# Talking-heads attention and a Fourier-mixing feed-forward: who issues the first loads, and the order of the first and last feed-forward units

## The chip, the cores and the metric

The kernel runs on one core of a Trainium2 chip. The metric is the device time of one execution in microseconds; the time of a kernel is the median of its runs.

## The reference

```python
# attention: 8 batches, 12 heads, 448 rows, 64 columns each
scores = scale * np.matmul(q, k.transpose(0, 1, 3, 2))
scores = np.einsum('bhij,hg->bgij', scores, w_pre)       # heads are mixed
attn = np.exp(scores - scores.max(-1, keepdims=True))
attn = attn / (attn.sum(-1, keepdims=True) + 1e-09)
attn = np.einsum('bhij,hg->bgij', attn, w_post)          # and mixed again
x = np.matmul(attn, v)                                   # to (8, 448, 768)
# Fourier mix and feed-forward
u = x + np.real(np.fft.fft(np.fft.fft(x, axis=1), axis=2))
un = (u - u.mean(-1)) / np.sqrt(u.var(-1) + 1e-06)
out = u + np.maximum(un @ w_ch1, 0.0) @ w_ch2            # 768 -> 3072 -> 768
```

All is float32; the two feed-forward weights come as 64-bit floats and are converted on the chip.

## The kernel before

**First phase (`mix_phase`).** Each batch is done in 23 steps, 184 in all; a step handles a few query rows of all 12 heads. Block by block (two or three steps a block), TensorE forms scores (`emit_qk`, "QK") out of transposed q and k (`emit_xpose`), one pair of head columns (`xx`) at a time, and ScalarE copies them to a tile `Sb` of which there are two. For each step, four DMAs gather rows of `Sb` into `Kr` (`emit_gather`, line 641), so that heads lie on partitions. TensorE mixes the heads (`emit_premix`), VectorE takes the maximum (`emit_max`), ScalarE the exponential (`emit_exp`), VectorE the reciprocal sum and GpSimd the scaling of `PP` (`emit_scale`, line 676); TensorE mixes again (`emit_postmix`), VectorE transposes to `Pv` (`emit_turn`), and TensorE multiplies by v (`emit_av`). Gathers run five steps ahead of the post-mix, premix to scaling two.

A list `fill` holds everything that is due at a step: `due(kind, at, fn)`. Steps below 0 are the prologue. The order of TensorE, VectorE, ScalarE and GpSimd in this phase is the order in which the program emits; SyncE mostly issues DMAs. Loads of the first batch (`b == 0`) are all due at step -40: for each of three pairs k, then q, each in four DMAs of 112 KB (line 570), two by SyncE and two by ScalarE, then v (line 579) by SyncE. Loads of later batches are GpSimd's, due at the steps of `AT_L` and `AT_V`. `emit_load_mix` loads the head-mixing weights `wrp` and a mask `mk`; `emit_mix` makes `kw1` and `kw2` of them.

The Fourier mix of a batch folds its rows on GpSimd (`fold`; tiles `xs`, `xq`, `xf`; lines 781 to 802) and finishes with small matmuls. Results are stored by closures that wait in a list `later`: some stores are indirect (line 864), and one of a single row follows (line 870). Converting the weights (`_Weights`; raw loads at line 232) is dealt out in small pieces (`wts.deal`) over all steps.

**Second phase (`ffn_phase`).** The 3584 rows are cut into 7 units of 512 rows, the hidden width into 6 parts, and each product is done in a seven-product scheme. For the first part, `first` computes the hidden values of a unit (line 1207, seven groups of 12 matmuls in the order of `ORDER`) and `second` multiplies by the second weights (line 1284) and adds to u. In between, the next unit is prepared: row statistics on VectorE (`stats`), their scales on GpSimd (`power`, four small operations on `mv`, lines 411 to 414), the normalization on ScalarE (`norm`, `un`, line 1136), transposes on TensorE (`turn`, line 1145). The unit n = 0 begins while the last pieces of the first phase are still done beside it (`next_part`, `fold_rest`). While unit 0 is emitted, GpSimd's order is the program's; from unit 1 on a scheduler places GpSimd's instructions.

For the other five parts, `second2` does each product once more in seven (line 1325) and adds quarters (128x192) of seven accumulators `D[j]` on ScalarE (copies, line 1353) and VectorE (adds, line 1347); whole accumulators are added to each other on 128x768 (`both`, line 1356) and go to `out` in DRAM by accumulating DMAs that GpSimd issues (`out_`, line 1359). In the very last unit (`end`) two quadrants of `out` are loaded into spare accumulators, completed there, and written by SyncE and ScalarE (`store`, line 1363). `on(s, fn)` places `fn` behind the s-th matmul pair of that list.

Of the kernel before, what the change touches and what calls it, by code (L numbers as in the profile page):

```python
# [16 lines left out]
P = 128  # L17
# [13 lines left out]
KR = R * NH  # L31
# [29 lines left out]
TOT = B * GS  # L61
# [27 lines left out]
AT_T = ((5, 9), (15, 16), (13, 15))  # L89
AT_L = ((-4, -3), (-2, -1), (0, 1), (2, 7), (10, 11), (12, 13))  # L90
AT_V = ((2, 3), (4, 5), (6, 7))
AT_QK = ((0, 2, 1), (0, 1, 2), (0, 1, 2), (1, 2, 2),
         (0, 1, 2), (0, 1, 2), (0, 1, 2), (0, 1, 2))
AT_AV = ((1, 2, 4), (0, 1, 3), (1, 3, 5), (1, 3, 4))
# [354 lines left out]
def mix_phase(ctx, tc, rest, ident, q, k, v, w_pre, w_post, u_scr, u_rev, wts, lead):  # L449
# [60 lines left out]
    def emit_load_mix():  # L510
        for t in dens:
            nc.gpsimd.memset(t[:, :, :], 1e-9)
        nc.gpsimd.memset(wrp[:, :, :], 0.0)
        nc.sync.dma_start(out=mk, in_=cn["mk"].ap())
        for x in range(2):
            for y in range(2):
                nc.sync.dma_start(
                    out=wrp[64 * x + 30 * y:64 * x + 30 * y + 30, 0, :],
                    in_=_ap(w_pre, 6 * y * NH, [[0, R], [NH, 6], [1, NH]]))
            nc.sync.dma_start(out=wrp[64 * x:64 * x + KR, 1, :],  # L520
                              in_=_ap(w_post, 0, [[0, R], [NH, NH], [1, NH]]))

    def emit_mix():
# [31 lines left out]
    def emit_load_qk(b, xx, nm, y):  # L555

        src = q if nm == "q" else k
        if y == 0 and b == 0 and xx == START[-1]:

            if "raw" not in first:  # L560
                first["raw"] = ppv.tile([P, GT, 2 * S], F32, name="Pv", tag="Pv")
            batches[b]["raw" + nm, xx] = first["raw"][:, nm == "q"].rearrange(
                "p (c x d) -> p c x d", c=C7, x=2)
        elif y == 0:
            batches[b]["raw" + nm, xx] = praw.tile([P, C7, 2, D], F32, name="raw" + nm,
                                                   tag="raw")
        t = batches[b]["raw" + nm, xx]
        for x in range(2):
            eng = nc.gpsimd if b else (nc.sync, nc.scalar)[x]
            eng.dma_start(  # L570
                out=t[64 * y:64 * y + 64, :, x, :],
                in_=src[b, 6 * y + 2 * xx + x].rearrange("(p c) d -> p c d", c=C7))
        return True

    def emit_load_v(b, pr, y):
        if y == 0:
            batches[b]["v", pr] = pvv.tile([P, 2, C7 * D], F32, name="vv", tag=f"vv{pr}")
        h = 6 * y + 2 * pr
        (nc.gpsimd if b else nc.sync).dma_start(
            out=batches[b]["v", pr][64 * y:64 * y + 64, :, :],  # L580
            in_=v[b, h:h + 2].rearrange("h (p c) d -> p h (c d)", c=C7))

# [49 lines left out]
    def emit_gather(T):  # L632

        Kr = pkr.tile([P, 2, S], F32, name="Kr", tag="Kr")
        n, j = at_step[T]
        Sb, rs = blocks[n]["Sb"], blocks[n]["rs"]
        row = _row(Sb)
        for z in range(2):
            for x in range(2):
                p0 = 64 - R * rs + 4 * j + 2 * z + x  # L640
                nc.sync.dma_start(
                    out=Kr[64 * x:64 * x + KR, z, :],
                    in_=_ap(Sb, p0 * row, [[rs * row, 2 * R], [S, 6], [1, S]]))
        steps[T]["Kr"] = Kr
# [242 lines left out]
    for b in range(B):  # L887
        f = b * GS
        at_t = [(a, nm, xx) for xx, at in enumerate(AT_T) for nm, a in zip("qk", at)]
        if b == 0:  # L890

            for i, xx in enumerate(START):
                for j, nm in enumerate("kq"):
                    for y in range(2):
                        due("none", -40, lambda xx=xx, nm=nm, y=y: emit_load_qk(0, xx, nm, y))
                    due("full", 2 * i + j - 20, lambda xx=xx, nm=nm: emit_xpose(0, xx, nm))
                for n in range(2):
                    due("QK", 2 * i + 2 + n - 20, lambda n=n, xx=xx: (emit_qk(n, xx), n))
            for pr in range(3):
                for y in range(2):  # L900
                    due("none", -40, lambda pr=pr, y=y: emit_load_v(0, pr, y))
        else:
            for at, (a, nm, xx) in zip(AT_L, sorted(at_t, key=lambda e: e[0])):
                for y in range(2):
                    due("none", f + at[y] - GS,
                        lambda b=b, xx=xx, nm=nm, y=y: emit_load_qk(b, xx, nm, y))
            for xx, at in enumerate(AT_T):
                for nm, a in zip("qk", at):
                    due("full", f + a - GS,
                        lambda b=b, xx=xx, nm=nm: emit_xpose(b, xx, nm))  # L910
        for pr in range(3 if b else 0):
            for y in range(2):
                due("none", f + AT_V[pr][y], lambda b=b, pr=pr, y=y: emit_load_v(b, pr, y))
        for n in range(0 if b else 2, NBL):
            for xx in range(3):
                due("QK", f + BLOCK_AT[n] - 8 + AT_QK[n][xx],
                    lambda n=NBL * b + n, xx=xx: (emit_qk(n, xx), n))
        for n in range(NG):
            for pr in range(3):
                due("AV", f + GROUP_AT[n + 1] + AT_AV[n][pr],  # L920
                    lambda a=b * NG + n, pr=pr: (emit_av(a, pr), None))
            at, gi = AT_X[n]
            if b == B - 1 and n > 1:
                at += 2
            due("full", f + at, lambda g=groups[b * NG + gi]: emit_x(g))
        for n, at in enumerate(AT_Z):
            due("full", f + at, lambda b=b, n=n: emit_z(b, n // 2, n % 2))
        for pair in range(2):
            for par in range(2):
                due("full", f + AT_S[pair][par],  # L930
                    lambda b=b, pair=pair, par=par: emit_s2(b, pair, par))
# [8 lines left out]
    due("none", f + 15, lambda: lead.power(lead.mv))  # L940
    due("none", f + 26, lambda: lead.total(0))
    due("none", 0, lambda: wts.deal(0))
    due("none", -39, emit_load_mix)
    due("none", -3, emit_mix)
    for at, t in ((9, (rows, "at", 0, PN)), (16, (ts, "ts", 0, PN)),
                  (17, (tcs, "tc", 0, CW // 2)), (19, (tcs, "tc", CW // 2, CW))):
# [21 lines left out]
    with tc.manual_schedule(engines={ET.PE, ET.DVE, ET.Activation, ET.Pool}):  # L968
        while s <= TOT - GS + AT_X[-1][0]:
# [3 lines left out]
            for op in ORDERS[s % 2]:  # L973
# [12 lines left out]
                elif op == "scale":  # L986
                    if ahead:
                        emit_scale(s + LM)
                    for _ in range(old):
                        later.pop(0)()  # L990

                    if s < TOT - 3:
# [43 lines left out]
TOTALS = ((4, 6, 0), (5, 2, 4), (6, 2, 6), (3, 1, 5))  # L1036
DEEP = 1
HALVES = {0: ((0, 0),), 1: ((1, 1), (2, 0)), 2: ((3, 1),), 3: ((4, 0),), 4: ((5, 1), (6, 0))}
DEALS = ((2, 2, 2, 2, 2, 0, 0), (3, 4, 4, 4, 3, 0, 0))
DEST = {0: (0, 0), 1: (0, 0), 4: (1, 1), 5: (0, 1), 2: (0, 1), 6: (1, 1), 3: (1, 0)}  # L1040
ACC = {0: "P", 5: "P", 6: "P", 3: "P", 1: "Q", 4: "R", 2: "R"}
# [3 lines left out]
def ffn_phase(ctx, tc, rest, ident, u_scr, u_rev, wts, ub_scr, out, fold_rest,  # L1045
# [135 lines left out]
    def first(n, st, beside):  # L1181
# [12 lines left out]
        for k, i in enumerate(ORDER):  # L1194
# [39 lines left out]
                nc.scalar.activation(h21, h21, ACTF.Relu)  # L1234
            else:
                nc.scalar.activation(h12, p, ACTF.Relu)
            x = k - 2 * (n == 0)
            if norms and 0 <= x < NT2:
                stats(t + 1, x)
                if x == NT2 - 1:  # L1240
                    power(t + 1)
            if (n == 0 and k < 2) or (n == 1 and k not in (1, 2)):
                next_part()
                if n == 0 and k == 1:
                    fold_rest(8)
            if n == 0 and k == 5:
                fold_rest()
            if deep:
# [22 lines left out]
    def second(t, st):  # L1271
# [6 lines left out]
        for k, i in enumerate(ORDER):  # L1278
# [18 lines left out]
                total(t + 1, k - NT2 + 1)  # L1297
            if t == 0 and k > 2:
                next_part()
            wts.deal(2 if norms and k >= NT2 else 4)  # L1300
            if t == NTB - 1:
                load_w2(1, i)

    def second2(n, st):
# [61 lines left out]
        for j, i in enumerate(ORDER2):  # L1366
# [7 lines left out]
                if key:  # L1374
                    on(b + s, take, j, q, key)
            on(b + 6, take, j, 0, "Q")
            on(b + 11, more, j, 3, "P")
            on(b + 16, more, j, 1, "R")
            if t == NTB - 1 and c + 1 < NC:
                on(b + 17, load_w2, c + 1, i)  # L1380
        j0, j3, j5, j6, j4, j1, j2 = range(7)
        v11, v12 = 7, 8
        pl = nc.gpsimd
        on(12, lambda: quarters(vec, st["hq"], st["h"], H21, H21 + 1))
        on(19, lambda: quarters(vec, st["hq"], st["h"], HS1, HS1 + 1))
# [1 line left out]
                                         st["h"][:, HS2], op=ALU.subtract))  # L1387
        on(20, lambda: quarters(pl, st["hq"], st["h"], H12S, H12S + 1))
        if end:
            for v, r, d in ((v11, 0, 0), (v12, 0, 1)):  # L1390
                on(0, load, v, r, d)
            on(27, out_, j3, 1, 0)
            for s, *o in ((24, vec, v11, j0), (33, vec, j5, j0), (34, pl, v12, j5),
                          (40, vec, j6, j5), (45, vec, v12, j4), (46, vec, j4, j6),
                          (52, vec, v11, j1)):
                on(s, both, *o)
            on(41, out_, j6, 1, 0)
            on(47, out_, j4, 1, 1)
            on(53, store, v11, 0, 0)
            on(61, store, v12, 0, 1)  # L1400
        else:
            for s, *o in ((33, j5, j0), (40, j6, j5), (47, j5, j4), (54, j0, j1),
                          (61, j5, j2), (62, j4, j6)):
                on(s, both, vec, *o)
            on(27, out_, j3, 1, 0)
            on(44, out_, j6, 1, 0)
            on(55, out_, j0, 0, 0)
            on(62, out_, j5, 0, 1)
            on(63, out_, j4, 1, 1)
# [14 lines left out]
    fold_rest()  # L1424
    parts_ = [(c, k) for c in range(1, NC) for k in range(NK + FM)]
    for n in range(NTB):
        if n:
            wts.add(*parts_.pop(0))
        wts.deal(0)
        if n + 2 < NTB:  # L1430
# [4 lines left out]
            for i in ORDER:  # L1435
                nc.sync.dma_start(out=ub_scr[0][i], in_=lead.ub[i])
        second(n, st)
        wts.deal(1000)
        if n == 0:
            order.close()  # L1440
            order.enter_context(tc.manual_schedule(engines={ET.PE, ET.DVE}))
# [100 lines left out]
```

## Time and profile before

| | us |
|---|---|
| median of 3 runs | 2321.06 |
| lowest, highest | 2319.83, 2324.16 |
| the profiled execution's own time | 2313.94 |
| span of its records | 2312.0 |

The profiled execution is 7.1 us below the median. The table of engines, in us of the span:

| engine | busy |
|---|---|
| TensorE (PE) | 2251.5 (97%) |
| VectorE (DVE) | 1719.8 (74%) |
| GpSimd (POOL) | 1277.2 (55%) |
| ScalarE (ACT) | 1170.2 (51%) |

A row of the timeline reads: start in us, length in us, engine, line, operation, what is written and read, how many, and in brackets how long the engine had been idle and what ended it. Rows with SPq or ACTq are DMA issues, whose length is that of the issuing. The attention steps and the Fourier mix run to some 808 us, the feed-forward from there to the end.

### The profile page before, as it was taken

The numbers are of one execution on the slowest core, as the hardware profiler recorded it, in microseconds if no ns is written. First come the engines' busy times: TensorE is split into PE (matmuls) and PEld (weight loads), VectorE is DVE, ScalarE is ACT, GpSimd is POOL, SyncE is SP. The second block draws the span as 40 slices with busy tenths as digits, with TensorE's granted clock in tenths as the row PEclk, the third lists the DMA queues.
The fourth block names the chain that finished last, engine by engine and source line by source line (L and its number), as shares of the span: only waits on it lengthen the run. The fifth ranks groups of instructions, "written<-read, shape, count | busy, mean of one in ns | idle before, by whom it ended". The sixth has DMA issues, their size and how long they took to land.

```text
span 2312.0 us, 60775 instructions
## 1 busy us (share of the span) xinstructions
PE 2251.5 (97%) x22894; PEld 1738.0 (75%) x22894; DVE 1719.8 (74%) x3628; ACT 1170.2 (51%) x3336; POOL 1277.2 (55%) x1784
## 2 busy tenths in 40 slices
PE   6999999999999999999999999999999999999998
PEld 2455555555555677676899999999999899999997
DVE  3878878888877857777777787878778877765545
ACT  4776767666676622221345445444444445434433
POOL 3587868878787632221555454556555645453333
PEclk9999999999999999999999999999999999999999
DMA  7575655657656375667777887878777977795664
GB/s 162 163 187 163 187 176 164 195 159 192 186 172 197 134 249 196 205 205 285 219 172 194 226 229 187 222 180 248 209 185 188 281 182 176 190 259 120 141 144 69
DMA packets 231904, 439.04 MB, mean 190 GB/s; under 512 B 39608, under 2 KB 154064, under 8 KB 231614
## 3 DMA queue, kind: packets, MB, share of 16 engines
q1 hardware_dynamic: 157902, 302.97, 38.1%
q0 software_dynamic: 67856, 130.43, 29.9%
q8 instruction: 183, 3.00, 0.6%
q10 hardware_dynamic: 5856, 1.77, 0.5%
q14 instruction: 107, 0.88, 0.1%
HBM read 212.76 MB, written 143.16 MB: 154 GB/s over the span
## 4 chain that ended last, share of the span: by engine, by line
PE 83%; POOL 4%; DVE 4%; DMA 3%; ACT 2%; issue 1%; SPq 1%; ACTq 0%; DVEq 0%; POOLq 0%
PE psP L1207 17%; PE psP L1325 13%; PE psR L1207 9%; PE psR L1325 7%; PE mx L652 6%; PE ms L716 5%; PE ms L624 5%; PE po L686 4%; PE psQ L1207 4%; PE psQ L1325 3%; PE psP L1284 3%; PE ms L841 2%; PE psR L1284 1%; DMA Kr<-Sb 1%; PE ms L598 1%
## 5 line engine op out<-in xcount | busy, mean ns | idle before, releaser
L1359 POOL DMA_DIRECT2D out_dram<-od x173 | 210.1, 1273 | 262.8 <-DVE od L1347 187.2
L676 POOL TENSOR_SCALAR PP<-PP,rcp 128x448 f32<-128x448 f32 x368 | 235.2, 649 | 194.5 <-DVE rcp L674 164.9
L666 ACT ACTIVATE PP<-mx,nmx 128x448 f32<-128x448 f32 x368 | 230.5, 632 | 169.4 <-DVE nmx L659 156.7
L659 DVE TENSOR_REDUCE nmx<-mx 128x1 f32<-128x448 f32 x368 | 212.5, 618 | 92.8 <-PE mx L652 89.3
L1170 POOL TENSOR_TENSOR hq<-h 128x128 f32<-128x128 f32 (+1 forms) x210 | 129.7, 618 | 256.9 <-ACT h L1229 124.2
L1353 ACT COPY od<-psP 128x192 f32<-128x192 f32 x488 | 156.4, 320 | 171.9 <-PE psP L1325 170.7
L1356 DVE TENSOR_TENSOR od<-od 128x768 f32<-128x768 f32 x210 | 201.3, 972 | 52.1 <-ACT od L1353 51.8
L624 PE MATMUL ms<-kT,qT 64*32 64x448 f32 (+1 forms) x3072 | 199.3, 548 | 13.7 <-ACT qT L487 6.1
L487 ACT COPY Sb<-ms 124x448 f32<-124x448 f32 (+1 forms) x384 | 184.7, 541 | 54.3 <-PE ms L624 26.6
L699 DVE STREAM_TRANSPOSE Pv<-po 128x896 f32<-128x896 f32 x184 | 203.7, 1107 | 5.8 <-PE po L686 5.2
L652 PE MATMUL mx<-Kr,kw 60*32 60x448 f32 x2944 | 195.0, 550 | 8.8 <-ACT PP L666 5.0
L686 PE MATMUL po<-PP,kw 60*32 60x448 f32 x2944 | 187.8, 539 | 2.8 <-issue 1.4
L716 PEld LDWEIGHTS ms<-Pv,vv 64*64 64x64 f32 x5376 | 137.6, 132 | 69.8 <-issue 45.7
L1207 PE MATMUL psP<-qs,w1t 128*128 128x256 f32 x744 | 179.1, 379 | 0.8 <-DVE h L1228 0.8
L1207 PE MATMUL psP<-ks,w1t 128*128 128x256 f32 x744 | 179.1, 379 | 0.1
L716 PE MATMUL ms<-Pv,vv 64*64 64x120 f32 (+1 forms) x5376 | 159.7, 263 | 0.6 <-DVE XT L749 0.4
L252 POOL TENSOR_SCALAR wst<-wst 128x256 f32<-128x256 f32 (+1 forms) x76 | 118.2, 1564 | 67.9 <-ACT wst L263 66.6
L1207 PEld LDWEIGHTS psP<-qs,w1t 128*128 128x128 f32 x744 | 139.4, 190 | 17.6 <-DVE h L1228 1.2
L1207 PEld LDWEIGHTS psP<-ks,w1t 128*128 128x128 f32 x744 | 139.4, 190 | 16.7 <-DVE u L1289 0.7
L1207 PE MATMUL psP<-ub,w1t 128*128 128x256 f32 x528 | 127.1, 379 | 1.1 <-DVE h L1228 1.1
L1228 DVE TENSOR_TENSOR h<-h,psP 128x512 f32<-128x512 f32 x42 | 28.8, 686 | 127.6 <-PE psP L1207 104.9
L1325 PE MATMUL psP<-w2t,hq 128*128 128x192 f32 x490 | 122.4, 332 | 1.2 <-DVE od L1347 1.2
(190 smaller groups left out, 5289.2 us busy)
## 6 DMA issues: line engine op xcount, KB each, us to landing
Kr<-Sb SPq DMA_DIRECT2D x736, 105.0 KB
out_dram<-od POOLq DMA_DIRECT2D x173, 384.0 KB, 6.3
qs<-ub SPq DMA_DIRECT2D x89, 384.0 KB
ks<-ub SPq DMA_DIRECT2D x88, 384.0 KB
ub<-ub SPq DMA_DIRECT2D x79, 384.0 KB
w1t<-w SPq DMA_DIRECT2D x42, 384.0 KB
w2t<-w SPq DMA_DIRECT2D x42, 384.0 KB
raw<-in_moe_w_ch_dram SPq DMA_DIRECT2D x32, 384.0 KB
```

The costliest lines, as they stand in the source:

```text
L624: nc.tensor.matmul(pss[x][o:o + hi - lo, :S], st["qT", xx][64 * x:64 * x + 64, y, lo:hi], st["kT", xx][64 * x:64 * x + 64, y, :], start=Tr ...
L652: nc.tensor.matmul(mx[x][64 * z + o:64 * z + o + 32, :S], kw1[64 * x:64 * x + KR, o:o + 32], Kr[64 * x:64 * x + KR, z, :], start=True, sto ...
L659: nc.vector.tensor_reduce(nmx[:, :], steps[T]["mx"][x][:, :S], axis=AX.X, op=ALU.max, negate=True)
L666: nc.scalar.activation(steps[T]["PP"][:, x, :], steps[T]["mx"][x][:, :S], ACTF.Exp, bias=steps[T]["nmx", x][:, :], accum_out=steps[T]["den ...
L676: nc.gpsimd.tensor_scalar(PP[:, x, :], PP[:, x, :], rcp[:, x:x + 1], 1.0, op0=ALU.mult, op1=ALU.mult)
L686: nc.tensor.matmul(po[o:o + 32, z, :S], kw2[64 * z:64 * z + KR, y, :], PP[64 * z:64 * z + KR, :, c * HS:(c + 1) * HS], start=True, stop=True)
L699: nc.vector.transpose(turned[a]["Pv"][:, j, :].rearrange("p (z s) -> p z s", z=2), steps[T]["po"][:, :, :S])
L716: nc.tensor.matmul(pss[y][64 * x:64 * x + 64, :nu * R], st["v", pr][64 * y:64 * y + 64, x, jb * D:(jb + 1) * D], _ap(Pv, 64 * y * rp + 32 ...
L1207: mm = nc.tensor.matmul(p[:, m, :], w1[i][:, kc, m * P:(m + 1) * P], ub[:, kc, :], start=i in (0, 4, 1)[:3 - seed] and m == kc == 0, stop= ...
L1325: nc.tensor.matmul(ps[j, key][:, :DQ], a, b, start=m in (0, 4), stop=True, skip_group_check=True)
L1356: eng.tensor_tensor(D[j][:, :, :], D[j][:, :, :], D[k][:, :, :], op=ALU.add)
L1359: nc.gpsimd.dma_start(out=acc[t, r, d], in_=D[j][:, :, :], accum_op=ALU.add)
```

## The change

It has three places.

1. *The first loads.* Of the first batch's q and k, ScalarE issues only its four DMAs of the first pair; its eight of the second and third pair are issued by GpSimd. The mixing weights are issued by GpSimd at step -13 instead of by SyncE at -39. For the first three steps, two of the four gathers (`x == 1`) are issued by GpSimd. v of the first batch is issued by GpSimd at steps -1 to 4, and q and k of the second batch at the steps of `AT_L1` instead of `AT_L`; all these stand behind GpSimd's first scaling in its queue.
2. *The first feed-forward units.* Late in the first phase closures in `later` are left for the second. Statistics of unit 1 are taken after groups 2, 3, 4 and 4 instead of 2 to 5; six folds instead of eight precede them on GpSimd. Unit 1's weight piece is added, and its loads begun, inside `second(0)`.
3. *The last unit.* The spare accumulators hold the quadrants (0,1) and (1,1) instead of (0,0) and (0,1); the quadrant (0,0) is completed by two accumulating DMAs, and full-tile sums are placed differently.

The number of matmuls and their order on TensorE are the same. On the queues: ScalarE has 8 DMA issues fewer, SyncE 6 of v, 7 of the mixing weights and 6 gathers fewer; GpSimd has all these more. On VectorE the only differences are one pair of statistics that moves ahead of the add of `h21`, and the tail of the last unit. On ScalarE the first `un` of unit 1 now stands ahead of the relu of `h21`.

```diff
+AT_L1 = ((-1, 0), (1, 2), (5, 6), (7, 8), (10, 11), (12, 13))
+AT_V0 = ((-1, 0), (1, 2), (3, 4))
...
-        nc.sync.dma_start(out=mk, in_=cn["mk"].ap())
+        nc.gpsimd.dma_start(out=mk, in_=cn["mk"].ap())
...
-            eng = nc.gpsimd if b else (nc.sync, nc.scalar)[x]
+            eng = nc.gpsimd if b else (nc.sync, nc.scalar if xx == START[0] else nc.gpsimd)[x]
...
-        (nc.gpsimd if b else nc.sync).dma_start(
+        nc.gpsimd.dma_start(
             out=batches[b]["v", pr][64 * y:64 * y + 64, :, :],
...
-                nc.sync.dma_start(
+                (nc.gpsimd if x and T < 3 else nc.sync).dma_start(
                     out=Kr[64 * x:64 * x + KR, z, :],
...
-    due("none", -39, emit_load_mix)
+    due("none", -13, emit_load_mix)
...
-                    for _ in range(old):
+                    for _ in range(old if s < TOT + 5 else 0):
                         later.pop(0)()
...
+STATS0 = {2: (0,), 3: (1,), 4: (2, 3)}
...
-            x = k - 2 * (n == 0)
-            if norms and 0 <= x < NT2:
-                stats(t + 1, x)
-                if x == NT2 - 1:
-                    power(t + 1)
+            for x in (STATS0.get(k, ()) if n == 0 else (k,)):
+                if norms and x < NT2:
+                    stats(t + 1, x)
+                    if x == NT2 - 1:
+                        power(t + 1)
...
-                    fold_rest(8)
+                    fold_rest(6)
...
-            wts.deal(2 if norms and k >= NT2 else 4)
+            if t == k == 0:
+                wts.add(*parts_.pop(0))
+                wts.deal(0)
+            if t:
+                wts.deal(2 if norms and k >= NT2 else 4)
...
-            on(b + 11, more, j, 3, "P")
+            on(50.5 if end and j == 6 else b + 11, more, j, 3, "P")
...
-            for v, r, d in ((v11, 0, 0), (v12, 0, 1)):
+            for v, r, d in ((v12, 0, 1), (v22, 1, 1)):
                 on(0, load, v, r, d)
+            on(24, out_, j0, 0, 0)
             on(27, out_, j3, 1, 0)
-            for s, *o in ((24, vec, v11, j0), (33, vec, j5, j0), (34, pl, v12, j5),
-                          (40, vec, j6, j5), (45, vec, v12, j4), (46, vec, j4, j6),
-                          (52, vec, v11, j1)):
+            for s, *o in ((33, vec, j5, j0), (34, pl, v12, j5), (41, vec, j6, j5),
+                          (41, pl, v22, j6), (51.5, vec, v12, j4), (59, vec, v22, j4)):
                 on(s, both, *o)
-            on(41, out_, j6, 1, 0)
-            on(47, out_, j4, 1, 1)
-            on(53, store, v11, 0, 0)
-            on(61, store, v12, 0, 1)
+            on(42, out_, j6, 1, 0)
+            on(51.5, out_, j1, 0, 0)
+            on(58, store, v12, 0, 1)
+            on(60, store, v22, 1, 1)
...
-        if n:
+        if n > 1:
             wts.add(*parts_.pop(0))
         wts.deal(0)
...
-        wts.deal(1000)
+        if n:
+            wts.deal(1000)
```

More of the change, by code (lines that the diff above doesn't have):

```diff
@@ L513, in emit_load_mix @@
         nc.gpsimd.memset(wrp[:, :, :], 0.0)
-        nc.sync.dma_start(out=mk, in_=cn["mk"].ap())
+        nc.gpsimd.dma_start(out=mk, in_=cn["mk"].ap())
         for x in range(2):
             for y in range(2):
-                nc.sync.dma_start(
+                nc.gpsimd.dma_start(
                     out=wrp[64 * x + 30 * y:64 * x + 30 * y + 30, 0, :],
                     in_=_ap(w_pre, 6 * y * NH, [[0, R], [NH, 6], [1, NH]]))
-            nc.sync.dma_start(out=wrp[64 * x:64 * x + KR, 1, :],
+            nc.gpsimd.dma_start(out=wrp[64 * x:64 * x + KR, 1, :],
                               in_=_ap(w_post, 0, [[0, R], [NH, NH], [1, NH]]))
@@ L578, in emit_load_v @@
         h = 6 * y + 2 * pr
-        (nc.gpsimd if b else nc.sync).dma_start(
+        nc.gpsimd.dma_start(
             out=batches[b]["v", pr][64 * y:64 * y + 64, :, :],
@@ L640, in emit_gather @@
                 p0 = 64 - R * rs + 4 * j + 2 * z + x
-                nc.sync.dma_start(
+                (nc.gpsimd if x and T < 3 else nc.sync).dma_start(
                     out=Kr[64 * x:64 * x + KR, z, :],
@@ L898, in mix_phase @@
                     due("QK", 2 * i + 2 + n - 20, lambda n=n, xx=xx: (emit_qk(n, xx), n))
-            for pr in range(3):
-                for y in range(2):
-                    due("none", -40, lambda pr=pr, y=y: emit_load_v(0, pr, y))
         else:
-            for at, (a, nm, xx) in zip(AT_L, sorted(at_t, key=lambda e: e[0])):
+            for at, (a, nm, xx) in zip(AT_L if b > 1 else AT_L1, sorted(at_t, key=lambda e: e[0])):
                 for y in range(2):
@@ L910, in mix_phase @@
                         lambda b=b, xx=xx, nm=nm: emit_xpose(b, xx, nm))
-        for pr in range(3 if b else 0):
+        for pr in range(3):
             for y in range(2):
-                due("none", f + AT_V[pr][y], lambda b=b, pr=pr, y=y: emit_load_v(b, pr, y))
+                due("none", f + (AT_V if b else AT_V0)[pr][y], lambda b=b, pr=pr, y=y: emit_load_v(b, pr, y))
         for n in range(0 if b else 2, NBL):
@@ L1381, in second2 @@
         j0, j3, j5, j6, j4, j1, j2 = range(7)
-        v11, v12 = 7, 8
+        v22, v12 = 7, 8
         pl = nc.gpsimd
```

## The prediction

> **What bounds the kernel now.** I read the page's engine line and chain first, then the timeline of the three places that the change touches, then stretches of the trace.
>
> ```profile
> PE 2251.5 (97%) x22894; PEld 1738.0 (75%) x22894; DVE 1719.8 (74%) x3628; ACT 1170.2 (51%) x3336; POOL 1277.2 (55%) x1784
> PE 83%; POOL 4%; DVE 4%; DMA 3%; ACT 2%; issue 1%; SPq 1%; ACTq 0%; DVEq 0%; POOLq 0%
> ```
>
> TensorE carries the chain for 83% of the span. A change that leaves the matmuls alone can win only where TensorE stands still: at the start, between the two phases, at the end. Stretches of the trace (from:to, length, then busy us of PE, PEld, DVE, ACT, POOL, granted clock, DMA share, GB/s) show where:
>
> ```profile
> 6.00:15.30 9.30, 3.41 (x14) 2.64 (x14) 1.63 (x2) 2.61 (x3) 4.42 (x6) 1.00 1.33 197
> 29.40:41.00 11.60, 6.79 (x64) 1.83 (x64) 3.36 (x11) 2.37 (x8) 2.67 (x4) 0.85 0.32 114
> 41.00:61.40 20.40, 17.72 (x260) 7.74 (x262) 12.59 (x25) 13.56 (x37) 11.04 (x17) 0.83 0.61 180
> 61.40:101.00 39.60, 39.33 (x867) 20.52 (x875) 30.82 (x69) 29.57 (x93) 23.74 (x41) 1.00 0.56 168
> ```
>
> From 61.4 us on TensorE is busy 39.33 of 39.60 us: a microsecond won before that point is kept. The timeline of the start:
>
> ```profile
> 11.03 1.57 ACTq L570 DMA_DIRECT2D Pv<-in_q_dram  x2
> 12.63 1.28 ACT L487 ACT_TABLE_LOAD   x1 [12.63 <-DMA rawq<-in_q_dram]
> 15.31 1.74 PE L624 MATMUL ms<-kT,qT 64*32 64x448 f32 x16 [5.21 <-ACT qT L487]
> 29.45 45.67 SPq L641 DMA_DIRECT2D Kr<-Sb  x52
> 40.98 0.97 ACT L487 COPY Sb<-ms 104x448 f32<-104x448 f32 x2 [3.44 <-DMA Kr<-Sb]
> ```
>
> ScalarE issues 12 loads until 12.6 us before its first copy; TensorE waits 5.21 us for it. Then SyncE issues row gathers back to back, and ScalarE waits 3.44 us for the twelfth. The timeline between the phases:
>
> ```profile
> 818.72 0.56 POOL L870 DMA_DIRECT2D v<-X  x1 [4.76 <-DMA v<-X,rows]
> 819.37 2.19 POOL L232 DMA_DIRECT2D raw<-in_moe_w_ch_dram  x4
> 821.58 1.96 POOL L781 TENSOR_TENSOR xs<-X 113x384 f32<-113x384 f32 x2
> 830.98 0.69 POOL L411 TENSOR_SCALAR mv<-mv 128x4 f32<-128x4 f32 x1
> 834.82 0.88 PE L1145 MATMUL psQ<-ident,un 128*128 128x128 f32 x6 [3.61 <-ACT un L1136]
> ```
>
> GpSimd is late with the row scales (mv), so the normalization (un) is late and TensorE idles 3.61 us. And the end:
>
> ```profile
> 2301.76 0.56 PE L1325 MATMUL psP<-w2t,hq 128*128 128x192 f32 x2 [1.21 <-DVE od L1347]
> 2303.11 0.96 DVE L1356 TENSOR_TENSOR od<-od 128x768 f32<-128x768 f32 x1
> 2304.39 1.01 PE L1325 MATMUL psP<-wt,h 128*128 128x192 f32 x2 [1.42 <-DVE od L1347]
> 2305.71 0.35 DVE L1347 TENSOR_TENSOR od<-od,psR 128x192 f32<-128x192 f32 x1
> ```
>
> VectorE's full-tile sums (0.96 each) stand ahead of the small adds for which TensorE waits twice.
>
> **The Trainium skill.** "DMA: Bandwidth & Descriptors", section "Issuing engines are not separate DMA queues": transfers of all issuers share the same 16 engines, and another issuer saves only issue time. The trace agrees: 197 GB/s from 3 to 9 us with two queues, 203 from 10.5 to 13.5 with three. Its section "Queues, rings and completion order" has each engine go round the queues packet by packet; in that second stretch GpSimd's queue moved 0.24 of 0.61 MB, 39%. "TensorE: Matmul & The Clock Gate", section "What's actually happening": after an idle window of about 3.4 us the clock is halved. The trace agrees: TensorE idles 3.2 us before 42.6 us, slightly under that, and the stretch from 42 to 48 us has a clock of 0.50. "ScalarE: Activation LUTs", section "What ACT_TABLE_LOAD costs": 1.28 us, as in the row above.
>
> **Part 1, the start.** ScalarE keeps 4 of its 12 loads, so its table load comes near 3.4 us, under the wait for the first pair's data: its 5.21 us wait goes. What is late next is the data. The first pair's eight loads land between 3.6 and 8.24 us by the trace's completion times, and the first scores (QK) could start 2.75 us after (transposes from 8.37, VectorE's copy ending at 10.57, ScalarE's 0.85 us copy): 11.0. But GpSimd now issues eight 112 KB loads of pairs two and three at about 0.72 us (x4 took 3.04 in the timeline) from about 1.5 us on. Its first packets came 2.5 us after an issue before, so from 3.9 us it takes some 39%. Of the pair's 917 KB, 363 had moved by then; 554 KB at 61% of 197 GB/s take 4.6 us instead of 2.8. Landing slips from 8.24 to 10.0, QK from 11.0 to **12.75: -2.55 us** against 15.31. Bounds: no sharing, 11.0 (-4.3); all of GpSimd's 917 KB first, 12.9 + 2.75 = 15.65 (+0.3). Pairs two and three land by about 12 to 17 us (2.75 MB at 197 GB/s from 2 us, plus 1.4 from last packet to completion); their transposes come at QK + 1.7 and later and don't wait. The 14.15 us from QK to the first gather (15.31 to 29.45) is ScalarE and TensorE work in unchanged order.
>
> SyncE loses six v loads (6.55 us of issue), seven small ones (21.05 to 27.1) and six gathers. The first two cost and win nothing: SyncE waits for 29.45 anyway. VectorE's wait for wrp (to 28.36) goes, but premix starts only at 32.05. GpSimd gains the small seven, covered by its 25.7 us idle before 38.1.
>
> Gathers: 12 issues at 0.81 us; the last landed at 40.84, 11.4 us after the first issue, of which 2.40 is transfer. Now SyncE issues six (4.9 us) and GpSimd six beside it (4.3 us at 0.72). A GpSimd issue-to-landing is 3.0 us at best (w<-wst, 128 KB) and 5.2 at worst (v<-X,rows): the sixth, issued at +3.6, lands at +6.6 to +8.8; I take +7.3. ScalarE's copies and the second exponential, at +12.4 before, come at +8.3: **-4.1 us** (bounds -4.8 and -2.6).
>
> After that v (six of 224 KB) and the second batch's eight q, k loads stand behind the scalings. Six of the q, k loads and v used to come before 27 us; now some 2.5 MB run beside the gathers for five steps. GpSimd then has 1.25 + 0.64 + 1.44 = 3.3 us a step, about a step's length; a scaling has 2 to 4 us before its post-mix, so I cost that at nothing. The gathers lose bandwidth: 45 to 57 us already ran at 191 GB/s, and the extra 1.3 MB is 7 us of DMA time, which SyncE's lead of 5 us and gathers issued three steps ahead largely hide. Against that the 3.2 us idle should go, and with it two steps at half clock (up to 2.7 us). I take **0**, bounds -2.7 and +5. AT_L1 moves the second batch's loads a few steps; the first transposition of them is at step 5, some 15 us after its load: nothing.
>
> **Part 2, between the phases.** The one-row store, with its 4.76 us wait, and four weight loads (2.19) go behind the folds, which can start when X is copied (816.4) instead of 821.58. Six folds (6.5 us) end at 823, the last two follow the scales. The statistics move one group earlier: both last ones follow the add at 823.56, two times 1.01 + 0.21, done at 826.7. GpSimd's four small operations (831.0 to 833.7, 2.7 us) then end at 829.4 and un at 830.5, before TensorE's group ends (831.2): -3.61. The extra statistics delay the h21 add by 0.6 us, and its relu now stands behind un on ScalarE, so HS1 is ready at 832.2 where TensorE wants it at 831.7: +0.5. **-3.1 us** (bounds -3.9 and -1.5). The weight loads come near 837 and are first used from 858 on: covered. The store's reader is a unit hundreds of us later. The removed deals had nothing queued; VectorE's order shows no weight operation moved.
>
> **Part 3, the end.** Two 0.96 sums into v11 become accumulating stores that GpSimd issues (1.2 us each, GpSimd being idle 2.3 and 1.6 us there); j6's sum goes to GpSimd (1.80 us, free from 2298.5 on); j4 is added into v12 and v22, both behind the small adds. Placing VectorE's rows in the new order: the add that frees the bank is done at 2300.6 instead of 2301.6, the last matmul starts near 2301.65 instead of 2304.39, and the last sum ends at 2304.4 instead of 2306.06: -1.66. The last four 384 KB transfers still drain at some 200 GB/s, so I take **-1.2** (bounds -1.7 and +0.3).
>
> **Sum:** -2.55 - 4.1 + 0 - 3.1 - 1.2 = -11.0 us against the profiled execution's 2313.94. The runs' median is 2321.06, 7.1 above it; I take the difference off the median: **2310.1**.
>
> **Rivals.** About 0.2% (4.6 us) is what a measurement can tell from no change.
> - *Larger gain:* no bandwidth lost by the first pair (-1.75) and the clock stays up (-2.7): 2305.6. For it: the 3.2 us idle that comes before the half clock is shortened. Against: 39% was measured.
> - *The start comes to nothing:* pair one lands as late as the bound (+0.3), gathers win 2.6 and the loads take 2.6 back; 2 and 3 remain: 2317, within 0.2%. That is also the case of late gathers on GpSimd's queue.
> - *Slower:* GpSimd's 2.5 MB go ahead of the gathers altogether. Place: 35 to 55 us, where ScalarE already waited 2.90 us for Kr at 53.59. Price: 13.4 us at 191 GB/s less 3.9 of such waits already there, plus four steps of 2.5 us TensorE work at half clock, +19.5: 2329.6. It decides from a loss of 15.6 us, so if the gathers get clearly less than half of the bandwidth; 39% for the other side speaks against.
>
> **Chances.** Forecast 0.65 (2306 to 2316), larger 0.17, nothing 0.12, slower 0.06. Faster 0.82, same 0.12, slower 0.06. Range 2304.0 to 2316.5: it leaves out slower, half of nothing, and the tail of larger.
>
> **What would show it.** Table load near 3.4 us; first QK at 11 to 14; ScalarE's wait for Kr near 40.98 gone or short; mv before 829.5 and no 3.6 us before psQ; the last VectorE row a full-tile sum, some 6.5 us before the end. Wrong if QK stays at 15, if waits for Kr exceed 6 us together before 60 us, or if the psQ wait remains.

## The result and the profile after

| | us |
|---|---|
| median of 14 runs of the changed kernel | 2317.55 (2313.74 to 2330.51) |
| median of 14 runs of the kernel before, same chip | 2320.91 (2314.89 to 2326.72) |
| ratio after/before | 0.9992, 95% interval 0.998 to 1.0003 |
| profiled execution after, and its span | 2318.12, 2316.3 |

The ratio amounts to 1.9 us (the two medians lie 3.4 us apart), with an interval from 4.6 us faster to 0.7 us slower: no difference that this measurement can tell, where 11.0 us had been forecast. From the page of the changed kernel, engines and chain:

```profile
PE 2254.1 (97%) x22894; PEld 1738.2 (75%) x22894; DVE 1720.3 (74%) x3626; ACT 1172.0 (51%) x3336; POOL 1300.5 (56%) x1813
PE 83%; DVE 5%; POOL 4%; DMA 3%; ACT 2%; issue 2%; SPq 1%; ACTq 0%; DVEq 0%; POOLq 0%
```

TensorE is the bound as before and does the same work (2254.1 us, 2251.5 before). What changed lies in the three places again. The start, in the timeline of the changed kernel:

```profile
3.44 1.28 ACT L489 ACT_TABLE_LOAD   x1 [3.44 <-issue]
12.19 1.74 PE L626 MATMUL ms<-kT,qT 64*32 64x448 f32 x16 [0.98 <-ACT qT L489]
25.99 38.04 SPq L643 DMA_DIRECT2D Kr<-Sb  x36
48.08 0.97 ACT L489 COPY Sb<-ms 124x448 f32<-124x448 f32 x2 [4.42 <-DMA Kr<-Sb]
61.16 0.97 ACT L489 COPY Sb<-ms 124x448 f32<-124x448 f32 x2 [7.91 <-DMA Kr<-Sb]
62.81 1.72 PE L654 MATMUL mx<-Kr,kw 60*32 60x448 f32 x12 [4.25 <-ACT PP L668]
```

The first three rows are a gain: scores (QK) at 12.19 us instead of 15.31, gathers from 25.99 instead of 29.45. The fourth step's exponential starts at 42.32 us instead of 49.34: seven microseconds ahead. The 3.44 us wait that stood at 40.98 us before is gone. Then ScalarE waits 4.42 and 7.91 us for gathered rows (Kr). Ahead of the same two copies it waited 2.90 and 0.95 us in the kernel before:

```profile
53.59 0.97 ACT L487 COPY Sb<-ms 124x448 f32<-124x448 f32 x2 [2.90 <-DMA Kr<-Sb]
59.72 0.97 ACT L487 COPY Sb<-ms 124x448 f32<-124x448 f32 x2 [0.95 <-DMA Kr<-Sb]
```

Stretches of the trace of the changed kernel (columns as in the prediction) show what TensorE loses there:

```profile
18.00:26.00 8.00, 5.71 (x78) 2.57 (x78) 4.00 (x16) 5.06 (x11) 0.00 (x0) 1.00 0.01 2
26.00:37.10 11.10, 6.64 (x60) 1.84 (x64) 2.17 (x6) 3.04 (x8) 4.58 (x9) 0.70 0.51 165
37.10:50.00 12.90, 10.47 (x176) 3.87 (x168) 8.07 (x16) 7.77 (x21) 12.76 (x19) 1.00 0.88 183
50.00:63.00 13.00, 7.04 (x107) 2.86 (x98) 5.29 (x10) 5.09 (x15) 3.70 (x6) 0.93 0.77 183
63.00:101.00 38.00, 37.73 (x771) 18.68 (x765) 28.14 (x62) 27.07 (x83) 27.07 (x45) 0.94 0.59 174
```

and of the kernel before:

```profile
18.00:26.00 8.00, 7.07 (x71) 3.28 (x70) 2.18 (x3) 4.34 (x9) 0.00 (x0) 1.00 1.14 215
50.00:63.00 13.00, 11.94 (x200) 5.26 (x200) 9.61 (x20) 8.93 (x25) 6.34 (x11) 1.00 0.59 171
```

From 50 to 63 us TensorE does 107 matmuls; in the kernel before it did 200 in the same stretch. The QK matmul that stood at 62.89 us before stands at 65.67: the whole lead is gone. And note the first row of each: from 18 to 26 us the DMA engines, busy with v before (share 1.14), now move nothing (share 0.01).

Between the phases, timeline of the changed kernel:

```profile
822.74 1.95 POOL L783 TENSOR_TENSOR xs<-X 113x384 f32<-113x384 f32 x2 [2.23 <-ACT X L489]
833.28 0.25 POOL L413 TENSOR_SCALAR mv<-mv 128x4 f32<-128x4 f32 x1 [4.12 <-PE psR L1207]
837.62 0.82 PE L1145 MATMUL psQ<-ident,un 128*128 128x128 f32 x6
```

GpSimd now waits for the statistics instead of being late, and TensorE's transposes have no wait. Counted from the first hidden matmul of unit 0 (808.92 before, 815.49 after) they start after 22.13 us instead of 25.90. And the end:

```profile
2301.95 1.81 POOL L1360 TENSOR_TENSOR od<-od 128x768 f32<-128x768 f32 x1 [0.90 <-DVE od L1360]
2304.60 2.44 POOL L1363 DMA_DIRECT2D out_dram<-od  x2 [0.84 <-DMA out_dram<-od]
2304.77 0.55 PE L1329 MATMUL psP<-wt,h 128*128 128x192 f32 x2
2306.45 0.95 DVE L1360 TENSOR_TENSOR od<-od 128x768 f32<-128x768 f32 x1
```

TensorE's two waits are gone and VectorE ends with a full-tile sum. But GpSimd issues its last two accumulating stores only at 2304.60 and 2305.48, the first after a wait for an earlier store's landing; the last store lands at 2314.61.

### The profile page after: what moved, and what is told of

Its sections match the earlier page's. It is cut to its first block, busy times and chain, and to the rows that moved or that the text cites. A ratio compares the mean times of both kernels' runs of the same rounds, so it can differ in the third digit from the quotient of the medians.

```text
span 2316.3 us, 60786 instructions
## 1 busy us (share of the span) xinstructions
PE 2254.1 (97%) x22894; PEld 1738.2 (75%) x22894; DVE 1720.3 (74%) x3626; ACT 1172.0 (51%) x3336; POOL 1300.5 (56%) x1813
## 4 chain that ended last, share of the span: by engine, by line
PE 83%; DVE 5%; POOL 4%; DMA 3%; ACT 2%; issue 2%; SPq 1%; ACTq 0%; DVEq 0%; POOLq 0%
PE psP L1207 17%; PE psP L1329 14%; PE psR L1207 8%; PE psR L1329 7%; PE mx L654 6%; PE ms L718 5%; PE ms L626 5%; PE po L688 4%; PE psQ L1207 4%; PE psQ L1329 3%; PE psP L1284 2%; DMA Kr<-Sb 2%; PE ms L843 2%; PE ms L600 1%; PE ms L827 1%
```

## Experiments

All kernels are built from the kernel before. Two marks on TensorE, whose order is the same in all of them, carry the comparison: mark A is the QK matmul at 62.89 us in the profile of before, mark B the one at 226.57, the twelfth of its group of 16. Inside that group TensorE pauses in every kernel. In the changed kernel and in the start alone the pause falls just ahead of the twelfth matmul, in all others two instructions or so behind it; the rows are of the changed kernel, then of the kernel before:

```profile
228.97 0.95 PE L626 MATMUL ms<-kT,qT 64*32 64x448 f32 x11
230.60 0.93 PE L626 MATMUL ms<-kT,qT 64*32 64x448 f32 x5 [0.68 <-issue]
226.16 0.95 PE L624 MATMUL ms<-kT,qT 64*32 64x448 f32 x14
228.08 0.91 PE L624 MATMUL ms<-kT,qT 64*8 64x448 f32 x2 [0.97 <-issue]
```

So for these two kernels mark B is taken at the eleventh matmul, ahead of the pause; elsewhere the eleventh and the twelfth start within 0.02 us of each other.

**The start alone** (`e1_start`): all of the change's first place, nothing of the others.

> The start of the change alone (which queues issue the first batch's q and k, the mix weights from GpSimd, half of the first three steps' gathers from GpSimd, v and the second batch's q and k behind the first scaling); seam and end as before. The mark is the QK matmul that starts at 62.89 us in the profile of before and at 65.67 us in that of after. Theory A: the start gains some 7 us by the fourth exponential (49.34 -> 42.32) and pays it all back by the mark, because the six loads of v (1.38 MB) now share the DMA engines with the gathers of the fifth to ninth step: mark 64 to 67 us, waits of TensorE for Kr over 6 us in all between 28 and 70 us, time between 1 us under before and 4 us over it. Theory B (that stretch of after was the chance of one execution): mark 56 to 60 us, time 4 to 7 us under before.

Measured: 2327.7 us, ratio 1.0027 (1.0016 to 1.0039): 6.3 us *slower*. Second exponential at 37.23 us, mark A at 66.20, TensorE's waits for Kr 4.7 us between 28 and 70 us (short of the 6 expected), and 5.1 more for exponentials, which come late behind ScalarE's own waits. The stretch was no chance of one execution (theory B falls), and theory A's upper end of 4 us was too low.

**v back at the head** (`e4_start_v_head`): the same with

```diff
-        nc.gpsimd.dma_start(
+        (nc.gpsimd if b else nc.sync).dma_start(
             out=batches[b]["v", pr][64 * y:64 * y + 64, :, :],
...
-                due("none", f + (AT_V if b else AT_V0)[pr][y], lambda b=b, pr=pr, y=y: emit_load_v(b, pr, y))
+                due("none", f + AT_V[pr][y] if b else -40, lambda b=b, pr=pr, y=y: emit_load_v(b, pr, y))
```

> The start of the change, but the six loads of v issued at the head again, by SyncE behind its twelve loads of q and k; second batch's q and k as in the changed kernel. Theory A: v runs in the stretch of 18 to 26 us in which the DMA engines have nothing to do in the changed kernel, and the gathers of 45 to 60 us keep their pace: mark 56 to 61 us, time 3 to 7 us under before. Rival C (what delays the gathers is GpSimd's issue of six of them in each of three steps, 3.3 us a step, and the scalings behind it): mark stays at 64 to 67 us and the time with that of the start alone. Rival D (v at the head holds up the last q and k loads): first QK matmul back at 14 to 16 us instead of 12.2.

Measured: mark A at 56.89 us, 9.3 us ahead of the start alone; first QK at 12.58, so the last q and k loads are not held up (rival D falls); GpSimd issues the same gathers, so they are not what delayed the others (rival C falls). The edit gives v another issuer as well as an earlier place; the run below with four of the six loads at the head speaks to that. Time 2319.72 us, ratio 0.9989 (0.9973 to 1.0004): the ratio amounts to 2.6 us under before, just short of what theory A named; its interval reaches to 6.3 and includes no change. Against the start alone the time is 8.0 us less, and those two intervals do not overlap.

**The seam alone** (`e2_seam`): the change's second place, nothing else.

> The seam alone (the stages of the first two feed-forward units reordered). In the profile of before the first psQ transposes of unit 0 start 25.9 us after its first hidden matmul (808.92 -> 834.82), in after 22.1 us (815.49 -> 837.62). Theory: this gain belongs to the seam's own order: 22 to 23 us here, time 3 to 4 us under before. Rival: it was bought by the later arrival at the seam (folds that had more time), then 25 to 26 us here and the time of before.

Measured: 2314.76 us, ratio 0.9978 (0.9964 to 0.9991), 5.1 us under before. Its timeline:

```profile
838.17 0.25 POOL L411 TENSOR_SCALAR mv<-mv 128x4 f32<-128x4 f32 x1 [4.14 <-PE psR L1208]
842.51 0.82 PE L1146 MATMUL psQ<-ident,un 128*128 128x128 f32 x6
```

The first hidden matmul is at 820.38, so the transposes start after 22.13 us, to the hundredth as in the changed kernel: the gain is the seam's own. The third group of transposes starts after 30.07 us here, against 33.28 in the profile of before and 34.92 to 36.36 in the five other kernels with the old seam.

**The end alone** (`e3_end`): the change's third place.

> The end alone (the last unit's order of sums and stores). From the last VectorE subtraction's release of GpSimd's copy (2291.92 us before, 2294.95 after) to the end of the span: 20.1 us before, 21.35 us after. Theory A: VectorE's last sum ends 1.3 to 2 us sooner after that mark, but two accumulating stores (2 x 786 KB) that are issued 0.9 us apart beside two plain ones put the last landing later: 21 to 21.6 us here, time 1 to 1.5 us over before. Theory B, that of the forecast: 18.9 us, time 1.2 us under before.

Measured: 2321.42 us, ratio 0.9997 (0.9986 to 1.0008), which excludes neither theory. The trace is clearer. From GpSimd's first of the last four copies on, VectorE ends after 12.39 us (14.06 before), the last landing comes after 20.06 us (18.0 before), the end of the span after 22.78. (The expectation gave 786 KB for a store; the trace has 384 KB.) The stores' cost, from the DMA view of the changed kernel between 2295 and 2317 us (queue, records, MB, share of the 16 engines; q0 holds the four accumulating stores, q1 and q10 the plain ones):

```profile
q0 software_dynamic: 1088, 1.57, 49.2%
q1 hardware_dynamic: 288, 0.39, 5.3%
q10 hardware_dynamic: 288, 0.39, 4.9%
```

By the time of the records, a megabyte of accumulating store takes 31% of the stretch, a megabyte of plain store 13%. The two kinds also differ in the queue that carries them, which is not separated here.

**Two controls of the start, by their profiles.** All gathers from SyncE (`e5_v_head_kr_sp`):

```diff
-                (nc.gpsimd if x and T < 3 else nc.sync).dma_start(
+                nc.sync.dma_start(
```

> As the start with v at the head, but all gathers from SyncE again, none from GpSimd. With the split the third exponential came at 39.65 us in the changed kernel against 45.13 before, and the mark (the QK matmul at 62.89 us before) at 56.89 us with v at the head. Theory A (the split is worth what the forecast gave it, some 4 us, and lasts): mark at 60 to 62 us here. Rival (from the mark's point of view the gathers catch up either way, since they are all bound by SyncE's 0.8 us apiece later): mark at 56 to 58 us.

And two of v's six loads left behind the scalings, by `pr > 1` in the two lines of the edit above (`e9_start_v_4_of_6`):

> The start of the change with four of v's six loads at the head on SyncE and two left behind the scalings on GpSimd. The mark was at 66.2 us with none of them at the head and at 56.9 with all six. Theory A (bytes in the gathers' window): each load there costs some 1.55 us, mark 59 to 61.5 us. Rival (what matters is that GpSimd has any v load to issue between two scalings): mark at 64 us or later.

Measured: mark A at 59.45 without the split, between the two expectations. With four of the six at the head it is at 58.83: theory A or a little better, and far from the rival's 64, though GpSimd again issues two loads of v between scalings. By mark B the two loads left cost 5.6 us of the 7.8 that all six cost (table below), with 17.1 us at half clock on the way, more than any other kernel; so one profile does not show that the cost grows evenly with the bytes. The single times of these two kernels, 2324.61 and 2325.46 us beside 2324.37 of before, tell nothing.

**Putting the parts together** (`e7_v_head_seam`): start with v at the head, and the seam.

> Start with v at the head, and the seam; the end as before. Theory A (the parts add: start with v at the head -2.6 us by its median, -6 by its mark; seam -5.1 by its median, -4.7 by its third transposes): 7 to 11 us under before, ratio 0.995 to 0.997. Rival (what the start gains is lost again in the mix stage, whatever is changed in it): 4 to 6 us under before, ratio 0.998.

Measured: 2311.37 us beside 2324.37 of before, ratio 0.9943 (0.9928 to 0.9958), 13 us under before. The rival falls: the parts add. They come to more than the 7.7 us of the two parts by themselves and than theory A's 11 us, but the intervals of the parts reach to 6.3 and 8.4 us, so this is no sign of a further gain.

**A mended end on top** (`e8_v_head_seam_end2`), against the end of the change:

```diff
-            on(27, out_, j3, 1, 0)
...
-                          (41, pl, v22, j6), (51.5, vec, v12, j4), (59, vec, v22, j4)):
+                          (41, vec, j3, j6), (41.5, pl, v22, j6), (51.5, vec, v12, j4), (59, vec, v22, j4)):
...
-            on(42, out_, j6, 1, 0)
+            on(41, out_, j3, 1, 0)
```

> As that kernel, with the end of the change mended: VectorE adds the last-but-two sum of quadrant (1,0) to the one before it (one full-tile sum, 0.95 us), so that quadrant takes one accumulating store instead of two, issued ahead of GpSimd's full-tile sum. From GpSimd's first copy of the last four to the last landing: 18.0 to 18.7 us in the old order, 19.6 and 20.1 in the new one. Theory A (the bytes in flight in the last 10 us and the wait for the earlier store's landing set the end): last landing at 16.5 to 18.3 us, time 1 us under that of the kernel with the old end. Rival (VectorE's extra sum holds up the last tiles): 18.5 to 20 us, time equal to or above it.

Measured: 2312.14 us, ratio 0.9948 (0.9936 to 0.9959). The last landing comes 18.82 us after the copy, against 18.0 to 18.65 in the old order and 18.40 for the change's own end in the next kernel, and VectorE ends after 13.85 us instead of 12.39. The rival is nearer: the extra sum costs VectorE what it saves the queue. No gain over the old end.

**The whole change with v at the head** (`e10_all_v_head`), and the split once more (`e11_v_head_seam_kr_sp`).

> The whole change, with one thing undone: v's six loads at the head again, on SyncE. Theory A (v's bytes in the gathers' window are the one term of the forecast's sum that took the gain): the whole change's 0.9992 becomes 0.9945 to 0.997, 7 to 12 us under before, and the mark (62.89 us before, 65.67 in the changed kernel) is at 56.5 to 59.5 us. Rival (the end of the change costs as much as it seems in the traces, and the parts do not add): ratio 0.9975 to 0.999, although the mark is early.

> Start with v at the head and the seam, but with every gather on SyncE: a second look at what the split of the gathers is worth. Theory A (it lasts, as forecast, 4 us): the TensorE instruction that stood at 222.33, 223.96 and 223.62 us in the three kernels with split gathers and v at the head comes at 226 us or later. Rival (the gathers catch up, since SyncE's issue of 0.81 us apiece is again what all steps wait for): 222.5 to 224.5 us, as in the one look so far (223.76).

Measured: the whole change with this one thing undone takes 2310.63 us beside 2323.29, ratio 0.9952 (0.9935 to 0.9969), 11.1 us under before, as theory A had it, with mark A at 56.10, a little ahead of its range; the rival falls. Its stretches:

```profile
18.00:26.00 8.00, 5.75 (x79) 2.57 (x78) 4.05 (x16) 5.06 (x11) 0.00 (x0) 1.00 0.47 110
37.10:50.00 12.90, 12.48 (x216) 5.44 (x208) 9.53 (x20) 9.92 (x27) 11.33 (x17) 1.00 0.70 196
50.00:63.00 13.00, 12.02 (x200) 5.24 (x195) 11.30 (x24) 8.61 (x23) 8.14 (x16) 1.00 0.60 178
```

v uses the stretch from 18 to 26 us, and TensorE does 416 matmuls from 37.1 to 63 us where it did 283 in the changed kernel. Without the split mark B is at 224.89, between its two expectations again (its single time is 2313.94 us). All marks, in us; the last column is the time between 26 us and mark B in which TensorE's granted clock was 0.50:

| kernel | v | 2nd exponential | mark A | mark B | half clock |
|---|---|---|---|---|---|
| before | head | 41.83 | 62.89 | 226.57 | 10.2 |
| seam alone | head | 41.55 | 65.67 | 228.81 | 13.7 |
| end alone | head | 42.25 | 63.77 | 228.62 | 13.7 |
| changed kernel | behind scalings | 37.13 | 65.67 | 229.38 | 13.7 |
| start alone | behind scalings | 37.23 | 66.20 | 230.99 | 13.7 |
| start, 4 of 6 at head | mixed | 37.22 | 58.83 | 227.96 | 17.1 |
| start, v at head | head | 36.90 | 56.89 | 222.33 | 6.8 |
| the same and seam | head | 37.16 | 57.49 | 223.96 | 10.2 |
| the same, mended end | head | 36.59 | 59.09 | 223.62 | 10.2 |
| whole change, v at head | head | 37.13 | 56.10 | 219.61 | 6.8 |
| v at head, no split | head | 38.37 | 59.45 | 223.76 | 6.8 |
| the same and seam, no split | head | 38.41 | 59.84 | 224.89 | 6.8 |

Each row is one profile. The three kernels whose start is the old one spread over 2.8 us at mark A and 2.2 us at mark B, so smaller differences between single rows are not read.

## Why the prediction was wrong

**The step that failed is "after that": v and the second batch's loads, costed at 0 with bounds -2.7 and +5.** By the means at mark B it cost 7.8 us: 230.2 with v behind the scalings (two kernels), 222.4 with v at the head and the gathers split (four). The timed runs agree: 8.0 us between the start alone and the start with v at the head, and 9.3 us (0.9992 and 0.9952) between the changed kernel and the whole change with v at the head; in neither pair do the intervals overlap. The bound was too tight as well. The loads of the second batch stand at the same steps in both kernels of each pair, so the cost is v's.

Two of the reasons given were wrong. One, used against the "slower" rival, is the share. "39% for the other side" was read from 10.5 to 13.5 us, where GpSimd's queue moved 98 records (those with data of 3 to 4 KB) beside 1502 of two other queues (those with data of 256 bytes): that share belonged to those loads and could not be carried to others. The DMA view of the changed kernel from 42 to 58 us (queue, records, MB, share of engines; then issues, with KB each and us to landing):

```profile
q0 software_dynamic: 604, 1.79, 57.6%
q1 hardware_dynamic: 627, 0.96, 31.7%
Kr<-Sb SPq DMA_DIRECT2D x12, 105.0 KB
vv<-in_v_dram POOLq DMA_DIRECT2D x4, 224.0 KB, 9.7
```

and the queues of the kernel before in the same stretch:

```profile
q1 hardware_dynamic: 1263, 1.95, 40.5%
q0 software_dynamic: 405, 1.03, 25.3%
```

With v at the head (the whole change):

```profile
q1 hardware_dynamic: 1217, 1.86, 38.9%
q0 software_dynamic: 365, 0.94, 21.3%
```

In the changed kernel the two queues passed nearly as many records each (604 to 627; in the start alone 638 to 753), but GpSimd's data records are of 3 to 5.4 KB and the gathers' of 1792 bytes. So the gathers got 35% of the bytes, and SyncE issued 12 of them in 16 us instead of 18. It is no rule of one record each: in the stretch that the prediction read, GpSimd's 98 records went beside 799 and 703 of the other two queues. This fits the Trainium skill's "DMA: Bandwidth & Descriptors", section "Queues, rings and completion order", which has each engine take turns between queues, a packet at a time; it doesn't say what this makes of bytes, and the prediction, which had cited it, took a measured share as a constant. By the trace's completion times (the middle one of each gather's) a gather issued at 48.3 us landed 12.0 us later, against 4.4 us before and 5.2 with v at the head and the seam.

The other is the cover. SyncE's lead "and gathers issued three steps ahead" were to hide 7 us of DMA time. The lead had just been gained: at the fourth exponential (42.32 us) the changed kernel was 7.0 us ahead, and at mark A nothing was left of it. The prediction's own price of 7 us for 1.3 MB was close to what came; hiding it was not. v's earlier place was cheap because nothing else wanted the DMA engines from 18 to 26 us.

The same term counted on the clock: two steps at half clock were to go, up to 2.7 us. They came back later. In the first row, of the changed kernel, TensorE does 48 matmuls at a clock of 0.50; in the second, with v at the head, 120 at full clock:

```profile
61.10:67.90 6.80, 5.09 (x48) 1.73 (x48) 2.90 (x7) 4.41 (x12) 3.28 (x5) 0.50 0.64 216
61.10:67.90 6.80, 5.72 (x120) 3.19 (x128) 3.92 (x10) 3.81 (x14) 3.94 (x7) 1.00 0.75 183
```

Ahead of mark B that makes 13.7 us at half clock with v behind the scalings, and 8.5 in the mean of the four with v at the head. Half of the difference, 2.6 us, is an estimate of the most that the clock can have in the 7.8. The prediction laid the half clock of before to 3.2 us of idle time; there the clock was 0.50 from 34.5 us, 2.4 us after TensorE had gone back to work, to 37.9, and again from 41.3, 1.9 us into that idle time, to 48.1. So the agreement with the idle time that it saw there is loose, and what sets these stretches is not shown here.

Its "slower" rival had this mechanism and place, and the right point of decision (gathers with clearly less than half), but priced it at +19.5 and gave it 0.06. Some 7.8 us of that came; of the 10 us that it put on half clock, 2.6 us at most.

**The other terms of the sum:**

- *First QK -2.55:* -3.1 (12.19). Right in mechanism and size; table load at 3.44 as foreseen.
- *Gathers split, -4.1:* mis-sized. With v at the head, the second exponential starts at 38.4 us without the split and at 36.6 to 37.2 with it: 1.4 us. At mark B the means differ by 1.9 (224.3 against 222.4), the ranges overlapping. The saving was below the bound of -2.6. The loads themselves came nearly as forecast: by their completion times the last of the twelve landed 8.0 us after the first was issued (7.3 forecast), against 11.4 without the split. What failed is the assumption that the second exponential follows that landing by 1.0 us. Beside GpSimd's gathers each of SyncE's took 2.8 to 4.3 us to land instead of 2.3 to 2.5, and the first exponential started at 33.6 to 34.1 us instead of 32.6. Then TensorE, without a pause from 31.4 us in the changed kernel, worked at half clock until 37.2. In the three kernels with v at the head where half clock lasted to between 36.3 and 37.1 us, the second exponential came 3.0 to 3.2 us behind the landing; in the one where it ended at 34.5, 2.3 us. How much each of the two causes took is not separated.
- *Start in sum, -6.65 without v:* at mark B -5.6 (222.4 against 228.0, the mean of three kernels with the old start).
- *Seam -3.1:* -3.8 at the first transposes and -3.2 at the third group against before's own profile, on which the forecast was worked out. That profile was a favourable one: the six old seams have a mean of 35.05 us at the third group and all new ones 30.1, which is -5.0. The timed runs say -5.1 (-8.3 to -2.1). The working held: no wait, scales before they are needed.
- *End -1.2:* not seen. VectorE did end 1.3 to 1.7 us sooner, as worked out, but the last landing, counted from the same TensorE matmul 62 us ahead of it, comes at 63.2 and 63.7 us (changed kernel, end alone) and 62.0 (whole change, v at head) against 61.6 to 62.3 with the old end: 0 to 1.7 us later. The step in doubt is the drain "at some 200 GB/s": the change has one accumulating store more, and these are the dear ones. That this alone delays the landing is argued, not shown, and timing can't tell this term from -1.2.

Put together, -5.6 + 7.8 - 5.0 and 0 to 1.7 give -2.8 to -1.1, inside the interval of the measured ratio; so does the sum of the three parts' own times, +0.5. The start alone came out at +6.3 us (3.7 to 9.1) where the marks give 2.2; that difference is open. Of the signs named in advance, the one for "wrong" fired: waits for Kr of over 6 us before 60 us (ScalarE's 4.42 and most of its 7.91).

## What to carry to other kernels

A transfer taken out of an idle stretch of the DMA engines does not become free because it is "behind" something: ask what shares the engines in its new place. A share of bandwidth that was measured beside other loads does not carry over: here the queue with the larger records got 65% of the bytes, where 39% had been taken. A lead of a few microseconds is a stock that can be spent once; cost what follows against it, not beside it. The version to keep is the change with v issued at the head again: 0.9952 (0.9935 to 0.9969) with the new end, 0.9943 (0.9928 to 0.9958) with the old one, which this measurement doesn't tell apart.

## What the runs showed of the hardware

- In one stretch of 16 us two loaded queues passed 604 and 627 records, but 1.79 and 0.96 MB: the larger records took the bytes. A gather issued there landed after 12.0 us, against 4.4 us in the kernel before.
- A 105 KB gather from `Sb` to `Kr` landed 2.3 to 2.5 us after its issue when SyncE alone issued gathers, 0.8 us apart. With GpSimd issuing as many beside it, SyncE's took 2.8 to 4.3 us and GpSimd's 2.0 to 3.3.
- Accumulating stores to DRAM, issued by GpSimd, took 2.4 times the DMA engines' time per byte of plain stores issued by SyncE and ScalarE (31% and 13% of the same stretch for a megabyte).
- The mean granted clock differs between executions of one kernel, and most of the spread of their times goes with it: in the changed kernel's 14 runs it lies between 0.992 (2330.5 us) and 0.996 (2313.7 to 2318.1), some 2.9 us for 0.001 by a straight line through them. The profile of before was one at 0.996, the one of the start alone at 0.992; this is why parts are compared at early marks and by medians, and not by the ends of single profiles.
